# A new order for all engines, planned for eight outstanding loads and stores

## The chip, the core and the metric

The kernel runs on one core of a Trainium2 chip. The core has five engines that each take their instructions strictly in order: TensorE (PE, matmuls, with its weight loads shown as PEld), VectorE (DVE), ScalarE (ACT), GpSimd (POOL) and SyncE (SP, which only issues transfers). Transfers (DMAs) are issued by SP, ACT or POOL and run beside the engines. The metric is the device time of one execution, in microseconds, as the median of several runs; lower is better.

## What is computed

Two operators in a row: causal attention with 16 beacon keys in front, then a feed-forward layer with an ELU.

```python
B, H, S, D, Nb = 8, 8, 576, 64, 16
k_all = concat([beacon_k, k], axis=2); v_all = concat([beacon_v, v], axis=2)
scores = q @ k_all.T / sqrt(D), causal after the beacons
a = exp(scores) / sum(exp(scores))
x = (a @ v_all).transpose(0, 2, 1, 3).reshape(B * S, H * D)      # 4608 x 512
h = x @ w_in                                                       # 512 x 2048
g = where(h > 0, h, exp(h) - 1)
out = g @ w_out                                                    # 2048 x 512
```

Inputs and output are float32; inside, the matmuls take bf16 or fp16.

## The kernel before

The eight batches of attention and the feed-forward layer are interleaved in one program. A batch has four pairs of heads. For a pair (numbers n = 4b + hp) the steps are:

- load k and q (`load_pair`, 288 KB each) or, from batch 3 on, whole rows of tokens (`load_tok`); load the values of the batch (`load_v`) and the beacons (`load_bk`);
- cast them to bf16 (`cast_pair`, on DVE, POOL or ACT) into one of two buffers `sb`;
- bring them into the form that the scores need: PE transposes (`do_T2` for batch 0, `do_T` for batches 1 and 2; tiles `tr2`, `tr`) with copies out on DVE or ACT, or DMA transposes issued by SP (`turn_tok`);
- scores on PE (`do_SC`, tile `sc`, two buffers), exponentials on ACT (`do_exp`, tile `et`), the causal mask on POOL (`do_mask`), value matmuls on PE (`do_AV`, tile `av`), division on DVE (`do_norm`), and the way back into the transposed x by PE (`do_xT`, tile `xt`) or SP (`turn_x`).

The feed-forward layer works through the 4608 tokens in tiles of 128, 128, 256 and then 512. For each tile, sixteen groups of up-projection matmuls (`do_mm1`, tile `hps`; fewer and wider groups cover the small tiles) are followed by the exponential on ACT (`do_e`), a clamp on POOL (`do_clamp`) and the ELU on DVE (`do_join`). The down-projection (`do_plain` for the first 512 tokens, then `do_M` with seven products in place of eight; tile `ops`) is copied out and stored by SP. Both weight matrices come in four pieces of 1 MB each, cast to fp16 by the transfer (`load_w`, issued by POOL, 512 KB as written).

The order of the instructions is not that of the source. Each step is an `Op` with an engine, a due time, a duration and what it needs. The class `Plan` plays through the whole program while it is being built (`Plan.run`), engine by engine in the order of the due times, lets an op wait for what it needs, and then emits the instructions in the order in which they began. Only this order reaches the chip; what waits for what is then held by semaphores. Three tables written out by hand feed it: `KEYS` (the due times), `ENGINES` (one letter for each op that may run on several engines: S, A, P, D for SP, ACT, POOL, DVE) and a few constants. Where PE has nothing to do in the first 30 us of the played time, the planner puts in a filler matmul (`do_fill`, tile `spare`, line L290).

For transfers the planner before knows 16 ring places for each of SP and ACT (`ringSP`, `ringACT`; a large transfer takes four or eight), three queues that share one transfer engine in turn, and a duration and a latency for each kind. The built program has a further rule, in both kernels: the loads and stores issued by SP and ACT take eight completion semaphores (lanes) in turn, in the order in which they are emitted, so the ninth waits at the head of its engine's queue until the first has landed. POOL's loads of the weights have lanes of their own.

Of the kernel before, what the change touches and what calls it, by code (L numbers as in the profile page):

```python
# [22 lines left out]
class Op:  # L23
    def __init__(self, eng, key, dur, fn, deps=(), take=(), give=(), mode=None, lat=0.03, queue=0, parts=1):
        self.eng, self.key, self.dur, self.fn = eng, key, dur, fn
        self.deps, self.take, self.give = [d for d in deps if d is not None], take, give
        self.mode, self.lat, self.queue, self.parts = mode, lat, queue, parts
        self.left, self.after, self.rest = 0, [], parts
        self.lock = fn is not None and (eng, getattr(fn, "func", fn).__name__) in SHARED


class Plan:
    MODE_COST, SLACK = 0.1, 0.1
    ENGS = "PE", "SP", "ACT", "POOL", "DVE"

# [3 lines left out]
    def add(self, *args, **kw):  # L39
        op = Op(*args, **kw)  # L40
        self.ops.append(op)
        return op

    def run(self):
# [15 lines left out]
        free = dict.fromkeys(todo, 0.0)  # L60
        free["DMA"] = 0.0
        mode, lines, turn, port = None, ([], [], []), 0, 0.0
        events, order, now, n_left, tick = [], [], 0.0, len(self.ops), 0
# [12 lines left out]
        while n_left:  # L76
# [11 lines left out]
            for eng, line in todo.items():  # L88
# [3 lines left out]
                if op.left or any(self.slots[t] < op.take.count(t) for t in op.take):  # L92
# [7 lines left out]
                line.pop()  # L100
                for t in op.take:
                    self.slots[t] -= 1
# [19 lines left out]
            while events and events[0][0] <= now + 1e-9:  # L122
# [3 lines left out]
                n_left -= 1  # L126
                for t in op.give:
                    self.slots[t] += 1
# [14 lines left out]
def kernel(  # L143
# [134 lines left out]
    with tc.tile_pool(name="psum", bufs=1, space=bass.MemoryType.PSUM) as psum:  # L278
# [4 lines left out]
            "st": 4, "sb": 2, "ringSP": 16, "ringACT": 16, "vst": 4,  # L283
# [32 lines left out]
        def load(key, dur, fn, deps=(), take=(), issue=0.47, units=1, fixed=True):  # L316
# [4 lines left out]
            ring = ["ring" + on] * units  # L321
            one = add(on, key, issue, fn, deps=deps, take=take + ring)
# [7 lines left out]
            return add("DMA", key, dur, None, deps=[issue], lat=2.1, give=ring, queue=0 if on == "SP" else 2, parts=2 * units)  # L330

        issues = {"SP": [], "ACT": [], "st": [], "vst": []}
        add("SP", -1e6, 0.8, None)
        add("PE", -1e6, 1.3, None, mode=0)

        bks = {}

# [8 lines left out]
        def load_pair(n, is_k, eng):  # L346
# [4 lines left out]
            eng = nc.scalar if n == 0 and not is_k else eng  # L351
# [336 lines left out]
        def do_store(s, m, halves):  # L688
# [12 lines left out]
            "SPSPAPADSPDDDADAADDASPDDDDADAASDDDDDDDDSSDDADDDAAAASPSDSPAPDSAPDDASSPDADSSDDDASSPDADSPSPADAPSPPS"  # L701
            "ADDDSSDDASSPDDSSPDAAAAAAAAPAPSADASPAPSSDSSPAPAPAAAAADAASSPSSPAAAAPAAPADSDAPAAADAASAPSSPAPAADSAPA"
            "DAPADSDSAAAASDSSPAPAAAAAPSPADAASASAAPASPAAPAAAAAASPSDDDAADADDDDDAADDDDADAADDDAAAADDDAAADDDDAADAD"
            "DDAADDDDDADAADDADDDDDDDA"
# [178 lines left out]
        def place(b, a):  # L883
            return 32 * (b - 1) + 8 * a + SHIFT[b]
# [350 lines left out]
```

## Time and profile before

| | |
|---|---|
| median of 3 runs | 351.3 us (350.16 to 351.71) |
| the profiled execution | 351.03 us |
| its span on the core | 349.3 us |
| granted clock of PE over the span | 1.0 |
| HBM read, written | 37.22 MB, 9.44 MB |
| fillers (L290) | 125 |

The profile lists each engine's busy time as a union of its instructions' spans. In rows of groups, the columns are the source line, the engine, the operation, out<-in with shapes, the count, then busy us and mean ns of one, then the idle time of the engine just ahead of them and what ended most of it. Matmuls are pipelined: one takes longer from start to end than the distance to the next, so PE's rate is read from the time that a row of many takes. In a timeline or a list of issues the first column is the start in us, the second the length, and the bracket at the end is the idle time before and what ended it; "SPq" is an instruction that issues a transfer. In the chain of waits each row is a start, a length and what the time was spent on.

### The profile page before, as it was taken

The numbers are of one execution on the slowest core, as the hardware profiler recorded it, in microseconds if no ns is written. First come the engines' busy times: TensorE is split into PE (matmuls) and PEld (weight loads), VectorE is DVE, ScalarE is ACT, GpSimd is POOL, SyncE is SP. The second block draws the span as 40 slices with busy tenths as digits, with TensorE's granted clock in tenths as the row PEclk, the third lists the DMA queues.
The fourth block names the chain that finished last, engine by engine and source line by source line (L and its number), as shares of the span: only waits on it lengthen the run. The fifth ranks groups of instructions, "written<-read, shape, count | busy, mean of one in ns | idle before, by whom it ended". The sixth has DMA issues, their size and how long they took to land.

```text
span 349.3 us, 9404 instructions
## 1 busy us (share of the span) xinstructions
PE 335.4 (96%) x3709; PEld 233.2 (67%) x3709; DVE 240.8 (69%) x468; ACT 216.7 (62%) x331; POOL 206.1 (59%) x372
## 2 busy tenths in 40 slices
PE   7989889999998999999999999999999999999996
PEld 5557787755553685667768887568665667666685
DVE  3456487767677867787777658576667696686872
ACT  2557888757767775866657668676785664352420
POOL 3398799766864886577448575375364574324310
PEclk9999999999999999999999999999999999999999
DMA  7999969999899898999899769947222410310113
GB/s 214 283 256 247 226 145 228 206 189 181 173 183 195 118 214 131 214 193 194 157 176 217 146 142 170 197 101 174 63 54 77 118 33 18 85 63 0 62 62 120
DMA packets 139400, 52.61 MB, mean 151 GB/s; under 512 B 119388, under 2 KB 135772, under 8 KB 139356
## 3 DMA queue, kind: packets, MB, share of 16 engines
q1 hardware_dynamic: 84405, 33.39, 44.1%
q10 hardware_dynamic: 50727, 14.42, 22.2%
q0 software_dynamic: 4224, 4.19, 7.6%
q8 instruction: 29, 0.48, 0.6%
q14 instruction: 15, 0.12, 0.1%
HBM read 37.22 MB, written 9.44 MB: 134 GB/s over the span
## 4 chain that ended last, share of the span: by engine, by line
PE 78%; DMA 8%; DVE 5%; POOL 4%; ACT 1%; issue 1%; SPq 1%; ACTq 0%; POOLq 0%; DVEq 0%
PE hps L581 31%; PE ops L651 26%; PE av L525 8%; PE sc L489 7%; DMA xT<-x 4%; PE ops L659 3%; DMA st<-in_q_dram 2%; DMA st<-in_k_dram 2%; PE spare L290 2%; POOL et L505 2%; PE tr L438 1%; POOL e L592 1%; DVE gt L599 1%; DVE t L617 1%; DVE x L541 1%
## 5 line engine op out<-in xcount | busy, mean ns | idle before, releaser
L592 POOL TENSOR_SCALAR e<-e 128x512 f32<-128x512 f32 x144 | 94.6, 661 | 90.8 <-ACT e L588 89.8
L581 PE MATMUL hps<-xT,w_in 128*128 128x512 f16 (+2 forms) x768 | 141.5, 326 | 0.5 <-DVE xT L304 0.3
L498 ACT ACTIVATE et<-sc 128x736 f16<-128x736 f32 (+4 forms) x128 | 109.6, 889 | 31.3 <-PE sc L489 21.0
L599 DVE SCALAR_TENSOR_TENSOR gt<-e,hps 128x512 f16<-128x512 f32 x144 | 96.4, 681 | 44.8 <-POOL e L592 44.4
L588 ACT ACTIVATE e<-hps 128x512 f32<-128x512 f32 x144 | 85.1, 600 | 64.6 <-PE hps L581 59.0
L581 PEld LDWEIGHTS <-w_in 128*128 128x128 f16 x768 | 66.4, 98 | 45.6 <-issue 4.5
L505 POOL TENSOR_SCALAR_AFFINE_SELECT et<-et 128x256 f16<-128x256 f16 (+4 forms) x160 | 72.5, 472 | 22.9 <-ACT et L498 22.0
L651 PEld LDWEIGHTS <-gt 128*128 128x128 f16 x640 | 61.2, 98 | 13.8 <-issue 1.0
L651 PE MATMUL ops<-w_out,gt 128*128 128x256 f16 x384 | 46.9, 273 | 0.0
L525 PEld LDWEIGHTS <-et 128*128 128x128 f16 (+1 forms) x992 | 36.6, 97 | 7.8 <-issue 2.2
L525 PE MATMUL av<-v,et 128*128 128x65 f16 (+1 forms) x992 | 40.3, 193 | 1.2 <-POOL et L505 0.6
L489 PE MATMUL sc<-qT,kT 64*128 64x80 bf16 (+3 forms) x704 | 36.4, 231 | 2.2 <-ACT et L498 2.1
L489 PEld LDWEIGHTS <-kT 64*128 64x128 bf16 x704 | 21.2, 95 | 19.5 <-issue 16.3
L541 DVE TENSOR_TENSOR x<-av,rl 128x256 f16<-128x256 f32 (+2 forms) x68 | 32.1, 471 | 2.3
L651 PE MATMUL ops<-t,gt 128*128 128x256 f16 x256 | 31.9, 273 | 0.0
L540 DVE RECIPROCAL rl<-av 128x4 f32<-128x4 f32 (+2 forms) x68 | 12.5, 184 | 27.7 <-PE av L525 27.4
L304 POOL CAST st<-st 128x1024 bf16<-128x1024 f32 (+3 forms) x25 | 24.4, 974 | 7.0 <-DMA st<-in_q_dram 5.6
L651 PEld LDWEIGHTS <-s 128*128 128x128 f16 x256 | 24.2, 98 | 4.8 <-DVE s L631 0.2
L684 DVE TENSOR_TENSOR osb<-ops,part 128x512 f32<-128x512 f32 (+1 forms) x27 | 17.0, 630 | 7.4 <-PE ops L651 5.7
L290 PE MATMUL spare<-t 128*128 128x256 f16 x125 | 19.3, 289 | 1.4 <-DVE t L1168 1.3
L651 PE MATMUL ops<-t,s 128*128 128x256 f16 x128 | 16.1, 272 | 0.0
L290 PEld LDWEIGHTS <-t 128*128 128x128 f16 x125 | 12.0, 103 | 6.1 <-issue 1.9
(53 smaller groups left out, 216.9 us busy)
## 6 DMA issues: line engine op xcount, KB each, us to landing
out_dram<-osb SPq DMA_DIRECT2D x32, 256.0 KB, 3.1
vst<-in_v_dram ACTq DMA_DIRECT2D x15, 256.0 KB, 4.6
st<-in_q_dram ACTq DMA_DIRECT2D x14, 256.0 KB, 4.3
st<-in_k_dram SPq DMA_DIRECT2D x10, 288.0 KB, 5.9
st<-in_q_dram SPq DMA_DIRECT2D x9, 288.0 KB, 6.2
st<-in_k_dram SPq DMA_DIRECT2D x10, 256.0 KB, 4.7
w_in<-in_moe_w_in_dram POOLq DMA_DIRECT2D x4, 512.0 KB, 10.3
w_out<-in_moe_w_out_dram POOLq DMA_DIRECT2D x4, 512.0 KB, 8.4
```

The costliest lines, as they stand in the source:

```text
L290: nc.tensor.matmul(out=spare[:, 0:2 * P], lhsT=ones[:, 0:P], rhs=ones, start=True, stop=True)
L304: eng.tensor_copy(out=out, in_=in_)
L489: nc.tensor.matmul(out=sc[:, h, o:o + w], lhsT=kT[D * h:D * h + D, keys_of(n, jc)], rhs=qT[D * h:D * h + D, q0:q0 + w], start=True, stop=T ...
L498: nc.scalar.activation(out=et[:, :, 0:w], in_=scs[n, u][:, :, 0:w], func=AFT.Exp, bias=0.0, scale=float(1.0 / (D ** 0.5)))
L505: nc.gpsimd.affine_select(out=et[:, :, c0:c0 + dw], in_=et[:, :, c0:c0 + dw], compare_op=ALU.is_ge, fill=fill0, base=q0 + NB - keys.start, ...
L525: nc.tensor.matmul(out=av[:, c:c + D + 1], lhsT=ets[n, cut.unit_of[jc, at]][0:m, h, col:col + P], rhs=v16[0:m, jc, 2 * hp + h, 0:D + 1], s ...
L541: nc.vector.tensor_tensor(out=x16s[b % 2][:, blks[0]:blks[0] + nb, P * hp:P * hp + P].rearrange("q i (h d) -> q i h d", d=D), in0=av[:, :, ...
L581: nc.tensor.matmul(out=hps[:, (hi - lo) * j + a - lo:(hi - lo) * j + b - lo], lhsT=w_in16[:, cc, P * fc:P * fc + P], rhs=xT[cc][:, a % RIN ...
L588: nc.scalar.activation(out=e, in_=hpss[tt, i], func=AFT.Exp, bias=0.0, scale=1.0)
L592: nc.gpsimd.tensor_scalar(out=e, in0=e, scalar1=1.0, scalar2=0.0, op0=ALU.min, op1=ALU.max)
L599: nc.vector.scalar_tensor_tensor(out=gt, in0=e, scalar=1.0, in1=h, op0=ALU.subtract, op1=ALU.max)
L651: nc.tensor.matmul(out=bank_of(s, m, slice(half, half + 1))[:, 0], lhsT=a[:, fc, P * half:P * half + P], rhs=B_OF[m][:, fc], start=(first ...
```

## The change

The planner gets the eight lanes, loses the rings, and its tables are written anew. `Plan` has `LANES = 8`; each issue on SP or ACT takes one lane (two where a beacon part is loaded by an instruction of its own) and may begin only when the next lanes in turn are free; the landing gives them back. Start times of the engines come from `BEGIN` in place of two dummy ops. The assumed durations of transfers are raised by some per cent and split finer. All loads of pairs may now go to SP or ACT (`fixed=False`), also those of pair 0, and the rule that loads of one issuing engine keep their order among themselves is dropped (only those that share a set of buffers still do).

```diff
 class Plan:
     MODE_COST, SLACK = 0.1, 0.1
     ENGS = "PE", "SP", "ACT", "POOL", "DVE"
+    BEGIN = {"PE": 1.3, "SP": 0.8, "ACT": 0.8}
+    LANES = 8
...
+    def add_dma(self, issue, lanes, key, dur, **kw):
+        op = self.add("DMA", key, dur, None, deps=[issue], **kw)
+        op.issue, issue.lanes = issue, lanes
         return op
...
-                if op.left or any(self.slots[t] < op.take.count(t) for t in op.take):
+                lanes = [(lane + i) % self.LANES for i in range(op.lanes)]
+                if op.left or any(busy[i] for i in lanes) or any(self.slots[t] < op.take.count(t) for t in op.take):
...
                 line.pop()
+                for i in lanes:
+                    busy[i] = True
+                op.lane, lane = lanes, lane + op.lanes
...
                 n_left -= 1
+                if op.issue is not None:
+                    for i in op.issue.lane:
+                        busy[i] = False
...
-            "st": 4, "sb": 2, "ringSP": 16, "ringACT": 16, "vst": 4,
+            "st": 4, "sb": 2, "vst": 4,
...
+        PAIR, VALS, TOKS, WTS = 0.85, (0.95, 1.4), 1.3, 3.4
...
-            eng = nc.scalar if n == 0 and not is_k else eng
...
         ENGINES = (
-            "SPSPAPADSPDDDADAADDASPDDDDADAASDDDDDDDDSSDDADDDAAAASPSDSPAPDSAPDDASSPDADSSDDDASSPDADSPSPADAPSPPS"
...
+            "ADSDSDSDSDASSDADDAAADAADDDDDDDDSAPADADDADASPDDADDDDSPSDSPSPSADSSDADDSSPDDDSSDADDSSDADASAAPSDSPSA"
...
         KEYS = [
...
-                gots.append(load(key, 0.8, partial(load_pair, n, is_k), deps=() if is_k or n == 0 else "last",
-                                 take=["st"] if is_k else [], issue=0.61, fixed=n == 0))
+                gots.append(load(key, PAIR, partial(load_pair, n, is_k), deps=() if is_k or n == 0 else "last",
+                                 take=["st"] if is_k else [], issue=0.61, fixed=False))
...
-            got = add("DMA", 0, 3.2, None, deps=[got], lat=2.1, queue=1, parts=8)
+            got = add("DMA", 0, WTS, None, deps=[got], lat=2.1, queue=1, parts=12)
...
-        plan.lines = [issues[line] for line in ("SP", "ACT", "st", "vst")]
-        last = add("DMA", 0, 0.7, None)
+        plan.lines = [issues[line] for line in ("st", "vst")]
...
-        last.deps.append(sorted(issues["SP"], key=lambda i: i.key)[2])
```

What this does to the built program, engine by engine:

| | before | after |
|---|---|---|
| fillers on PE | 125 | 106 |
| of these, ahead of the first transposes | 26 | 41 |
| loads issued by ACT | 67 | 25 |
| loads and stores issued by SP | 105 | 147 |
| DMA transposes issued by SP | 80 | 80 |
| pairs of batch 0 loaded ahead of the first values | 2 | 4 |
| POOL: what stands ahead of the first piece of w_in | two pair casts, three value casts, a mask | two pair casts |
| POOL: order of the weight pieces | w_in, w_in, w_out, w_in, w_in, w_out x3 | w_in x4, w_out x4 |
| PE: score pairs, value matmuls and transposes ahead of the first up-projection | those of batch 0 nearly whole and some of batch 1 | a part of those of batch 0 |

The first loads stand so in the new program. SP: beacon k, k of a second pair, beacon k, q and k of the first pair, q of a fourth, values. ACT: k and q of a third pair, q of the second, then a cast of the beacon keys, k of the fourth pair. DVE's first cast is that of the pair whose q and k SP issues fourth and fifth.

More of the change, by code (lines that the diff above doesn't have):

```diff
@@ L59, in run @@
             line.reverse()
-        free = dict.fromkeys(todo, 0.0)
+        free = {e: self.BEGIN.get(e, 0.0) for e in todo}
         free["DMA"] = 0.0
+        busy, lane = [False] * self.LANES, 0
         mode, lines, turn, port = None, ([], [], []), 0, 0.0
-        events, order, now, n_left, tick = [], [], 0.0, len(self.ops), 0
+        events, order, now, n_left, tick = [(t, -1, None) for t in sorted(set(self.BEGIN.values()))], [], 0.0, len(self.ops), 0
         def arrive(o):
@@ L314, in movable, with load @@
             return op
-        def load(key, dur, fn, deps=(), take=(), issue=0.47, units=1, fixed=True):
+        def load(key, dur, fn, deps=(), take=(), issue=0.47, parts=2, lanes=1, fixed=True):
             deps = [issues["new"]] if deps == "last" else deps
@@ L320, in load @@
             fn = partial(fn, eng)
-            ring = ["ring" + on] * units
-            one = add(on, key, issue, fn, deps=deps, take=take + ring)
+            one = add(on, key, issue, fn, deps=deps, take=take)
             if not fixed:
@@ L329, in load @@
             issues["vst" if "vst" in take else "st"].append(issue)
-            return add("DMA", key, dur, None, deps=[issue], lat=2.1, give=ring, queue=0 if on == "SP" else 2, parts=2 * units)
+            return plan.add_dma(issue, lanes, key, dur, lat=2.1, queue=0 if on == "SP" else 2, parts=parts)
         issues = {"SP": [], "ACT": [], "st": [], "vst": []}
-        add("SP", -1e6, 0.8, None)
-        add("PE", -1e6, 1.3, None, mode=0)
         bks = {}
+        PAIR, VALS, TOKS, WTS = 0.85, (0.95, 1.4), 1.3, 3.4
         def load_bk(b, eng):
@@ L925, in plan_v @@
                 key = load_key(f"v{NKC * b + jc}", place(b - 1, 1.8 + 0.4 * jc))
-                got = load(key, 0.85 if b < NV and jc < NKC - 1 else 1.3, partial(load_v, b, jc), take=["vst"], issue=0.95 if jc == 0 or jc == 1 and b < NV else 0.48, units=4 if b < NV and jc < NKC - 1 else 8, fixed=False)
+                got = load(key, VALS[0] if b < NV and jc < NKC - 1 else VALS[1] if jc < NKC - 1 else VALS[1] * 0.65, partial(load_v, b, jc), take=["vst"], issue=0.95 if jc == 0 or jc == 1 and b < NV else 0.48,
+                           lanes=2 if jc == 0 or jc == 1 and b < NV else 1, parts=8 if b < NV and jc < NKC - 1 else 16, fixed=False)
                 v_cast[b, jc] = movable(
@@ L951, in plan_tok @@
                         s = add("SP", (place(b, DMA_AT[1]) + i), 1.25, partial(turn_tok, b, is_k, c + j),
-                                deps=[cast] + last_SC.get(b - 2, []), take=ring4)
-                        turned[b].append(add("DMA", place(b, DMA_AT[1]) + i, 0.6, None, deps=[s], give=ring4, lat=2.1, parts=8))
+                                deps=[cast] + last_SC.get(b - 2, []))
+                        turned[b].append(plan.add_dma(s, 1, place(b, DMA_AT[1]) + i, 0.6, lat=2.1, parts=8))
                     add("NONE", 0, 0.0, None, deps=turned[b][-m:], give=["sb"], lat=0.0)
@@ L1032, in plan_pair @@
                         for blk in blks:
[L1033 removed]
+                            s = add("SP", (at(AT[7])), 1.25, partial(turn_x, b, blk), deps=part.pop(blk))
                             turns.setdefault(b, []).append(s)
[L1035 removed]
+                            done = plan.add_dma(s, 1, at(AT[7]), 0.6, lat=2.1, parts=8)
                             last_X.setdefault(b, []).append(done)
@@ L1158, in plan_super @@
                         freed[mate] = got
-                        st = add("SP", k + 0.1, 0.47, partial(do_store, s, m, halves), deps=[got], take=["ringSP"])
-                        gone.append(add("DMA", k + 0.1, 0.75 if half is None else 0.38, None, deps=[st], give=["ringSP"], lat=2.1 if half is None else 2.0, parts=2))
+                        st = add("SP", k + 0.1, 0.47, partial(do_store, s, m, halves), deps=[got])
+                        gone.append(plan.add_dma(st, 1, k + 0.1, 0.75 if half is None else 0.38, lat=2.1 if half is None else 2.0, parts=2))
                     chain.append(got)
```

18 lines of the change are left out of this document (9 added, 9 removed), and 338 rows, old and new, of the table KEYS.

## The prediction

> **What bounds the kernel now.** I read the busy shares first, then the slices, then TensorE (PE) stage by stage, then the chain of waits of the first stage, then the queues that feed it. From the page:
>
> ```profile
> span 349.3 us, 9404 instructions
> PE 335.4 (96%) x3709; PEld 233.2 (67%) x3709; DVE 240.8 (69%) x468; ACT 216.7 (62%) x331; POOL 206.1 (59%) x372
> ...
> DMA  7999969999899898999899769947222410310113
> ```
>
> PE is busy 96% of the span and no other engine passes 69%. DMA is near full for the first half and idle for the last third. By stages (columns after the stretch: its length, then busy time and count of PE, PEld, DVE, ACT, POOL, then clock, DMA share, GB/s):
>
> ```profile
> 0.00:6.92 6.92, 4.47 (x26) 3.20 (x26) 1.48 (x7) 1.28 (x1) 2.56 (x17) 1.00 0.63 186
> 6.92:36.70 29.78, 26.98 (x367) 19.15 (x368) 17.14 (x45) 17.92 (x25) 20.88 (x31) 1.00 1.12 265
> 36.70:70.00 33.30, 30.25 (x527) 25.70 (x524) 23.62 (x59) 27.09 (x41) 28.19 (x49) 1.00 1.00 199
> 70.00:346.20 276.20, 273.68 (x2797) 185.16 (x2794) 198.55 (x360) 170.18 (x266) 154.42 (x277) 1.00 0.68 132
> ```
>
> From 70 us on PE idles 2.5 of 276 us: there is nothing to win there and, if loads come late, something to lose. Everything open lies before 70 us. The same view for the filler matmuls alone (line L290, which keep PE turning while data is on its way):
>
> ```profile
> 0.00:6.92 6.92, 4.47 (x26) 3.20 (x26) 1.00 0.63 186
> 6.92:36.70 29.78, 14.81 (x99) 8.75 (x99) 1.00 1.12 265
> ```
>
> All of PE's work before 6.92 us is filler, and of the 367 matmuls up to 36.70 us, 99 are. So the start is a wait for data. The chain of waits of this stage (start, length, what):
>
> ```profile
> 0.84 3.33 DMA st<-in_k_dram
> 4.18 8.09 DMA st<-in_q_dram
> 12.35 0.77 DVE st L304
> ...
> 14.86 1.42 PE spare L290 x12
> ...
> 24.45 0.55 PE sc L489 x8
> ...
> 26.88 0.29 PE sc L489 x10
> ...
> 27.38 0.50 PE tr L438 x9
> ```
>
> The first link is a load, the second a load that was issued only when the first had landed (0.84 + 3.33 = 4.17; issue at 4.18). That is the limit the change is about: there are eight completion lanes, and the ninth load or store of SP and ACT waits at the head of its queue until the first is in. The issues show it (start, length of the issue):
>
> ```profile
> 1.25 0.74 SPq L352 DMA_DIRECT2D st<-in_k_dram  x1
> 2.04 0.62 SPq L352 DMA_DIRECT2D st<-in_q_dram  x1
> ...
> 4.18 0.61 SPq L352 DMA_DIRECT2D st<-in_q_dram  x1
> 8.44 0.60 SPq L352 DMA_DIRECT2D st<-in_k_dram  x1
> ```
>
> SP stands from 4.79 to 8.44. The old plan did not know this limit, so its order was made for loads that come earlier than they do.
>
> **The change, part by part.** No operation of the result is added or removed; what changes is every engine's order, the number of fillers (125 to 106), and who issues loads (ACT 67 to 25, SP's loads and stores 105 to 147, SP's transposes 80 in both).
>
> *Where the first up-projection stands.* Before it, the old order has 106 value matmuls (av), 28 more transposes than the new one, and 12 score matmuls of 256 columns, 4 of 240 and 20 of 80 more; the new one has 32 av there. By the chain's rows 28 transposes at 0.50/9 = 0.056 are 1.6 us, 16 wide scores at 0.55/8 = 0.069 are 1.1, 20 narrow ones at 0.29/10 = 0.029 are 0.6; 74 av at the rate of a full group are 2.2:
>
> ```profile
> 291.47 1.46 PE av L525 x48
> ```
>
> ```profile
> 36.71 0.28 PE L581 MATMUL hps<-xT,w_in 128*128 128x128 f16 x2
> 68.54 1.03 PE L581 MATMUL hps<-xT,w_in 128*128 128x256 f16 x8
> ```
>
> The last two rows are the old first and sixteenth group of up-projections. 5.5 us of real work are left for later, so the new kernel breaks even if its first up-projection starts at 36.7 - 5.5 = 31.2 us, as long as the rest runs as closely packed. Now when does it start?
>
> *The first data.* The new order begins with three whole pairs of k and q, spread over both queues; VectorE's first cast wants the pair that SP issues fourth and fifth, 928 KB into SP's queue (32 + 288 + 32 + 288 + 288). What the old trace shows of landings, by the casts that waited for them:
>
> ```profile
> 6.11 0.76 DVE L304 CAST st<-st 128x1152 bf16<-128x1152 f32 x1 [4.51 <-DMA st<-in_q_dram]
> ...
> 6.93 0.68 PE L448 MATMUL tr<-identb,st 128*128 128x128 bf16 x9 [1.20 <-DVE st L304]
> ...
> 8.55 1.14 POOL L304 CAST st<-st 128x1152 bf16<-128x1152 f32 x1 [5.25 <-DMA st<-in_q_dram]
> ...
> 10.24 0.61 POOL L304 CAST v<-vst 128x512 f16<-128x512 f32 x1 [0.54 <-DMA vst<-in_v_dram]
> ...
> 11.51 0.61 POOL L304 CAST v<-vst 128x512 f16<-128x512 f32 x1 [0.66 <-DMA vst<-in_v_dram]
> ```
>
> SP's 608th KB was in at 8.55, its 864th at 11.51, ACT's 832nd at 10.24. The new pair's 928 KB on SP stand beside 864 KB on ACT, so 11.5 is the upper end if the queues share as before and 10.2 the lower; I take 11.0, then 0.76 for the cast: first transposes at about 11.9, against 6.93 now. Fillers cover only part: 26 took 4.47 us (cold), 15 more at 1.42/12 = 0.118 end at 7.5 us, then PE stands for 4.4 us. That loss is wanted: the second, third and fourth pair are then in or nearly in, whereas the old kernel waits for each in turn (8.55 and 12.35 us).
>
> *From the first transposes to the first up-projection.* ACT sets this. In the new order ACT copies, then runs nine exponentials of batch 0 before the score pair whose last part stands just ahead of the up-projection.
>
> ```profile
> 7.70 0.45 ACT L302 ACTIVATE qT<-tr 128x256 bf16<-128x256 bf16 x1 [5.61 <-PE tr L451]
> ...
> 10.90 0.97 ACT L498 ACTIVATE et<-sc 128x960 f16<-128x960 f32 x1 [2.41 <-POOL v L304]
> 12.86 1.94 ACT L498 ACTIVATE et<-sc 128x1024 f16<-128x1024 f32 x2 [0.98 <-PE sc L489]
> ...
> 18.38 1.02 ACT L498 ACTIVATE et<-sc 128x1024 f16<-128x1024 f32 x1 [0.71 <-PE sc L489]
> ```
>
> First exponential 3.2 us after the first transposes (two pairs are cast and transposed by then, and three copies like the first row go ahead on ACT). Then four of 0.97, five of 1.0, two q copies and one xT copy between them (1.3 in all), and 0.8 for a wait where a pair of score tiles needs both buffers. The rows show 0.71 to 0.98 for each such wait; there are three places, and I count one, since in the others ACT still works on the tile before when the first of the pair is written. 3.9 + 5.0 + 1.3 + 0.8 = 11.0; 3.2 before and 0.9 after it for narrow scores and four fillers make 15.1 us from the transposes, near 27.0. I add 1.2 for hand-overs that I did not count, about 0.1 us at each of a dozen steps: 28.2. Bounds: 26.0 (data at 10.2, no slip) and 31 (data at 11.5, slip of 3).
>
> *The weights.* GpSimd issues the first two pieces of w_in after its two casts (1.14 each, from 12.8 on): 15.2 and 16.1 us, now 19.48 and 20.97.
>
> ```profile
> 19.48 0.90 POOL L430 DMA_DIRECT2D w_in<-in_moe_w_in_dram  x1
> ...
> 20.97 0.76 POOL L430 DMA_DIRECT2D w_in<-in_moe_w_in_dram  x1
> ```
>
> ```profile
> w_in<-in_moe_w_in_dram POOLq DMA_DIRECT2D x4, 512.0 KB, 10.3
> ...
> st<-in_q_dram SPq DMA_DIRECT2D x9, 288.0 KB, 6.2
> ```
>
> At 10.3 us to landing, piece one is in at 25.5, before the start at 28.2. A further one follows each 2 to 5 us (512 KB at the 199 to 265 GB/s of the stages, alone or with one other queue), about as each is used. Pieces three and four stand behind masks on GpSimd, hence the slip above; if that cover is gone, every us is paid.
>
> *Up-projections 1 to 16.* The old kernel goes from its first group to its sixteenth in 31.8 us. In the new order PE has 25.5 us of work between first and sixteenth (counted as above, the groups at 0.9 us), ACT 16 exponentials of L588 and 12 of L498.
>
> ```profile
> L498 ACT ACTIVATE et<-sc 128x736 f16<-128x736 f32 (+4 forms) x128 | 109.6, 889 | 31.3 <-PE sc L489 21.0
> L588 ACT ACTIVATE e<-hps 128x512 f32<-128x512 f32 x144 | 85.1, 600 | 64.6 <-PE hps L581 59.0
> ```
>
> 16 x 0.600 + 12 x 0.889 = 20.3, with copies 23. Old PE idle in that stage was 33.30 - 30.25 = 3.1 us; I take the same, so 28.6 us with ACT at 80%, where it now has 27.09 of 33.30 = 81%. Ends: 0 (ACT at 90%) and 6.
>
> *Issues moved from ACT to SP.* 42 x 0.61 = 25.6 us leave ACT's queue over the run, hidden now by ACT's 38% idle time; worth 0, at most 1. On SP a load then stands behind transposes and stores that wait; SP idles most of the run, but what is queued behind a waiting transpose is late by that wait. I take 0 from 70 us on, ends -1 and +3.
>
> **Sum.** 28.2 - 31.2 = -3.0 us; later stages 0; tail of the last supertile the same order of matmuls and stores. The profiled execution took 351.03 us (349.3 of span and 1.7 around it), the runs' median is 351.3: 351.03 - 3.0 = 348.0.
>
> **A rule against it.** The Trainium skill, "SBUF — State Buffer", in its box on VectorE blocking a DMA, says that a load issued from GpSimd is starved while VectorE runs copies in a fast mode. No run here shows that lock by itself, but the 10.3 us to landing for 512 KB of w_in against 6.2 for 288 KB on SP leave room for it; the new order issues w_in amid VectorE's copies too.
>
> **The rivals.**
>
> *A, slower: the start moves as a whole.* SP, VectorE and GpSimd each take things in order. If the pair on SP's queue lands at 13 instead of 11, the cast of a pair that is long in (6.11 in the old trace) waits behind it, the exponentials start 2 us later, GpSimd's casts too, and with them w_in, which stands behind those casts. Priced: start at 31.2 + 2.5 = 33.7, 353.5 us. It decides as soon as the first up-projection starts after 31.2. For it: the first transposes do come 5 us later by my own sum, with the 15.1 us of ACT behind them. Against it: 11.5 is a measured landing for nearly as many bytes. 0.23.
>
> *B, given back on ACT.* PE and ACT have almost equal work in the sixteen groups, so each wait of one is a wait of the other. If ACT gets only 73% full, between the 81% there and the 17.92 of 29.78 = 60% of the stage before, they take 31.5 instead of 28.6 us: 348.0 + 2.9 = 350.9, no change. For it: the new order has no attention of batch 1 to fill in with as early. Against: ACT is freed of load issues. 0.14.
>
> *C, the plan decides little.* If DMA volume alone sets the time up to 70 us, since its share is 1.0 to 1.2 there, both orders end where the bytes do: 351.0. Against: the share was 0.63 in the first 6.92 us, and which bytes come first is what PE waits for. 0.05.
>
> *D, the clock.* The first 26 fillers took 0.17 us each and later ones 0.118, though the clock column says 1.00. If PE's 4.4 us of standing slows it again, the next transposes and scores (some 2 us) take twice as long, half of it on the path: 349.0. 0.05. The Trainium skill, "TensorE: Matmul & The Clock Gate", Part 1, says that about 3.4 us without work halves the clock; by that rule D happens.
>
> **How the numbers follow.** Forecast 0.53 (own range 345 to 349.5), A 0.23, B 0.14, C 0.05, D 0.05. About 0.5%, 1.8 us, is what a measurement tells from no change. Faster: 0.53 and D, 0.58. Same: B and C, with a little of A, 0.21. Slower: the rest of A, 0.21. The range reaches from 344.0 (start at 26, some of the 3.1 us idle saved) to 354.0 (A).
>
> **What would show it.** First transposes near 11.9 and not before 10.9; ACT's first exponential near 15; first up-projection at 28.2, before 31.2; PE idle time from there to the sixteenth group near 3 us; 106 fillers; after 80 us PE never idle for long, and the last stage as long as now. Wrong if PE waits for w_in at the first up-projections, if the first cast ends after 13 us, or if new gaps on PE after 70 us exceed 3 us in all.

## The result, and the profile after

The changed kernel is slower. Its median is 361.1 us (360.33 to 361.64, 4 runs) against 351.3 us for the kernel before (350.16 to 351.71, 3 runs; a fourth took 483.65 us and is left out as slow). The recorded ratio is 1.0301, with a 95% interval from 1.0267 to 1.0335; the two medians alone give 1.028. The profiled execution took 361.64 us, 359.7 of them in the span. The page of the changed kernel, lines as shown of before, with the granted clock and the two hardware queues (q1 is SP's, q10 ACT's):

```profile
span 359.7 us, 9342 instructions
...
PE 337.4 (94%) x3690; PEld 233.3 (65%) x3690; DVE 237.6 (66%) x466; ACT 219.4 (61%) x335; POOL 199.1 (55%) x370
...
PEclk9999999999999989999699999999999999999999
DMA  7899928999799999899989799744403300220213
...
q1 hardware_dynamic: 117973, 42.34, 58.1%
q10 hardware_dynamic: 17159, 5.47, 8.0%
```

Two slices of the clock line are below 9, one from 126 us on and one from 171 us on; in the kernel before none was. The stages of the changed kernel (columns as in the prediction: length, then PE, PEld, DVE, ACT, POOL, clock, DMA share, GB/s), cut at its first transposes and its first up-projection:

```profile
0.00:10.67 10.67, 7.17 (x41) 5.22 (x42) 1.48 (x7) 1.91 (x2) 2.56 (x17) 1.00 0.79 237
10.67:29.39 18.72, 16.64 (x195) 10.96 (x196) 12.11 (x32) 12.07 (x18) 16.08 (x22) 1.00 1.06 203
...
90.00:130.00 40.00, 34.20 (x393) 21.64 (x392) 26.38 (x54) 28.03 (x41) 23.69 (x47) 0.96 1.03 169
130.00:190.00 60.00, 56.88 (x649) 37.42 (x648) 39.52 (x77) 40.03 (x60) 38.27 (x73) 0.94 1.04 170
190.00:359.00 169.00, 163.96 (x1623) 116.87 (x1620) 115.36 (x206) 91.78 (x146) 79.47 (x147) 1.00 0.45 99
```

PE alone, in the kernel before, over nearly the same stretches:

```profile
90.00:130.00 40.00, 38.48 (x439) 1.00 0.96 173
130.00:190.00 60.00, 59.54 (x656) 1.00 1.02 183
```

The start came out near the forecast, the stretch from 90 to 190 us did not: PE stands for 8.9 us there (40.00 - 34.20 + 60.00 - 56.88), where it stood for 2.0, and its clock falls.

PE's order can be followed as work done: count its matmuls in order, without fillers, at their undisturbed rate, and read when each kernel has done so many us of them. The table is worked out from the two traces in this way.

| PE's work done, us | before, at us | after, at us | after is ahead by |
|---|---|---|---|
| 40 | 64.8 | 61.5 | 3.3 |
| 70 | 94.8 | 91.2 | 3.6 |
| 90 | 116.4 | 114.2 | 2.2 |
| 100 | 126.1 | 128.0 | -1.9 |
| 140 | 165.5 | 166.6 | -1.1 |
| 150 | 174.9 | 183.6 | -8.7 |
| 310 | 331.8 | 341.1 | -9.3 |

The change wins 3.6 us at the start and loses 12.9 behind it, 4.1 at one place and 7.6 at another. These are the two places in the timeline (start, length, instruction, and the idle time before it with what ended it):

```profile
121.50 1.04 PE L664 MATMUL ops<-t,gt 128*128 128x256 f16 x8
124.75 2.46 PE L594 MATMUL hps<-xT,w_in 128*128 128x512 f16 x8 [2.21 <-DVE gt L612]
...
171.04 0.52 PE L502 MATMUL sc<-qT,kT 64*128 64x256 bf16 x14
174.29 1.09 PE L538 MATMUL av<-v,et 128*128 128x65 f16 x12 [2.73 <-DVE gt L612]
...
123.38 0.72 DVE L320 CAST st<-st 128x1024 bf16<-128x1024 f32 x1 [5.26 <-DMA kT<-st]
124.02 1.87 DVE L612 SCALAR_TENSOR_TENSOR gt<-e,hps 128x512 f16<-128x512 f32 x3
...
172.32 0.61 POOL L320 CAST st<-st 80x512 bf16<-80x512 f32 x1 [3.18 <-DMA kT<-st]
172.90 1.19 POOL L605 TENSOR_SCALAR e<-e 128x512 f32<-128x512 f32 x2
...
173.54 1.29 DVE L612 SCALAR_TENSOR_TENSOR gt<-e,hps 128x512 f16<-128x512 f32 x2 [5.26 <-POOL e L605]
```

Read from the bottom of each: PE waits for a join (`gt`) on DVE. At 124 us three joins stand behind a cast of tokens; at 173 us the join waits for a clamp on POOL that stands behind such a cast. The cast waits for a DMA transpose to land, which gives back one of the two `sb` buffers. Behind each wait PE has work again but at a lower clock:

```profile
118.00:122.00 4.00, 3.64 (x31) 1.00 1.28 173
122.00:126.00 4.00, 1.79 (x11) 0.99 0.95 192
126.00:130.00 4.00, 4.00 (x18) 0.58 0.75 154
...
172.00:176.00 4.00, 1.49 (x15) 0.71 0.85 170
176.00:180.00 4.00, 4.00 (x29) 0.50 1.04 209
180.00:184.00 4.00, 4.00 (x68) 0.93 0.77 174
```

PE's busy time in these six rows by what the clock lacks of 1.00 comes to 4.4 us, most of it 4.00 x 0.42 and 4.00 x 0.50. So the wait of 2.21 us was followed by 1.7 us lost to the clock, the one of 2.73 us by 2.7 us.

### The profile page after: what moved, and what is told of

It reads as the page before. It is cut to its first block, busy times and chain, and to the rows that moved or that the text cites. A ratio compares the mean times of both kernels' runs of the same rounds, so it can differ in the third digit from the quotient of the medians.

```text
span 359.7 us, 9342 instructions
## 1 busy us (share of the span) xinstructions
PE 337.4 (94%) x3690; PEld 233.3 (65%) x3690; DVE 237.6 (66%) x466; ACT 219.4 (61%) x335; POOL 199.1 (55%) x370
## 4 chain that ended last, share of the span: by engine, by line
PE 65%; DMA 17%; DVE 5%; SPq 3%; POOL 2%; issue 2%; ACT 1%; ACTq 0%; POOLq 0%; DVEq 0%
PE hps L594 27%; PE ops L664 21%; DMA kT<-st 6%; PE av L538 6%; PE sc L502 5%; PE ops L672 4%; DMA st<-in_q_dram 4%; DMA vst<-in_v_dram 3%; DMA xT<-x 2%; DVE gt L612 2%; SPq L400 2%; DMA out_dram<-osb 1%; DMA st<-in_k_dram 1%; POOL et L518 1%; PE tr L451 1%
## 5 line engine op out<-in xcount | busy, mean ns | idle before, releaser
L605 POOL TENSOR_SCALAR e<-e 128x512 f32<-128x512 f32 x144 | 92.8, 649 | 87.1 <-ACT e L601 85.8
L511 ACT ACTIVATE et<-sc 128x1024 f16<-128x1024 f32 (+4 forms) x128 | 109.4, 889 | 38.2 <-PE sc L502 28.9
L601 ACT ACTIVATE e<-hps 128x512 f32<-128x512 f32 x144 | 83.9, 600 | 60.5 <-PE hps L594 55.2
L518 POOL TENSOR_SCALAR_AFFINE_SELECT et<-et 128x256 f16<-128x256 f16 (+4 forms) x160 | 70.5, 460 | 33.3 <-ACT et L511 31.6
L664 PEld LDWEIGHTS <-gt 128*128 128x128 f16 x640 | 62.1, 99 | 13.3 <-issue 1.5
L538 PEld LDWEIGHTS <-et 128*128 128x128 f16 (+1 forms) x992 | 36.8, 98 | 10.3 <-issue 5.2
L664 PE MATMUL ops<-t,gt 128*128 128x256 f16 x256 | 32.7, 282 | 0.1
L320 POOL CAST st<-st 128x1024 bf16<-128x1024 f32 (+3 forms) x21 | 19.4, 924 | 21.9 <-PE tr L464 8.1
L306 PE MATMUL spare<-t 128*128 128x256 f16 x106 | 17.6, 306 | 3.3 <-DVE t L1182 1.3
L320 DVE CAST st<-st 128x1152 bf16<-128x1152 f32 (+3 forms) x12 | 8.6, 726 | 14.1 <-DMA st<-in_k_dram 8.3
## 6 DMA issues: line engine op xcount, KB each, us to landing
w_out<-in_moe_w_out_dram POOLq DMA_DIRECT2D x4, 512.0 KB, 12.9
```

The source lines that it names most:

```text
L306: nc.tensor.matmul(out=spare[:, 0:2 * P], lhsT=ones[:, 0:P], rhs=ones, start=True, stop=True)
L320: eng.tensor_copy(out=out, in_=in_)
L511: nc.scalar.activation(out=et[:, :, 0:w], in_=scs[n, u][:, :, 0:w], func=AFT.Exp, bias=0.0, scale=float(1.0 / (D ** 0.5)))
L518: nc.gpsimd.affine_select(out=et[:, :, c0:c0 + dw], in_=et[:, :, c0:c0 + dw], compare_op=ALU.is_ge, fill=fill0, base=q0 + NB - keys.start, ...
L538: nc.tensor.matmul(out=av[:, c:c + D + 1], lhsT=ets[n, cut.unit_of[jc, at]][0:m, h, col:col + P], rhs=v16[0:m, jc, 2 * hp + h, 0:D + 1], s ...
L601: nc.scalar.activation(out=e, in_=hpss[tt, i], func=AFT.Exp, bias=0.0, scale=1.0)
```

## The experiments

Four theories were told apart: **S**, SP's queue is too full, since 42 loads moved to it; **C**, casts that wait hold up joins and clamps in order; **D**, the 16 DMA engines are full from 60 us on and the new order has left them work undone; **B**, two buffers are too few. These letters are not those of the prediction's rivals. All ratios are against the kernel before, run on the same chip; the changed kernel itself stands at 1.030.

### Loads moved back from SP to ACT, and the reverse

The order on every engine and the plan stay; only the issuing engine of 39 loads is another (names: q, k or v, batch, block).

```diff
+        MOVED = "q34 k31 k32 k34 q40 q41 q42 q43 k44 q51 q53 q54 k51 k54 q60 ... v70 v71 v74".split()
...
-            fn = partial(fn, eng)
+            fn = partial(fn, nc.scalar if name_of(fn) in MOVED else eng)
```

> The changed kernel, its plan and the order on every engine kept, but the 39 loads of batches 3 to 7 that the change moved from ACT's queue to SP's are issued on ACT again. Theory S (a filled SP queue makes the DMA transposes, then the casts that wait for a buffer, then the joins late): SP's issue time from 118 to 163 us falls from 20 to about 15 of every 20 us, the gaps of PE at 122 and 171 us (2.5 and 2.9 us) are gone and the clock stays at 1.00 behind them: 349 to 353 us, since the start's lead of 3.5 us is kept. Rival T (the casts that the change put on DVE in batch 4, or the eight-lane bound, are the cause): the gaps stay, 359 to 362 us. Rival A (ACT is now the engine that is short): new gaps of PE that end on exp or e of ACT, 355 us or more.

357.8 us, ratio 1.0208 (1.0154 to 1.0262): three of the ten us come back, less than S said. The wait at 171 us is gone; at 121 us PE still stands, for another reason:

```profile
118.30 0.84 ACT L520 ACTIVATE et<-sc 128x800 f16<-128x800 f32 x1
122.22 0.39 ACTq L397 DMA_DIRECT2D st<-in_q_dram  x1
122.66 1.08 ACT L610 ACTIVATE e<-hps 128x512 f32<-128x512 f32 x2 [3.52 <-DMA out_dram<-osb]
```

A load at the head of ACT's queue waits until a store has landed; that the two share a lane is read from the eight-lane rule. The exponential behind the load, which is in no need of that, waits 3.5 us too. So a load is not free on ACT either.

> As the run before it, but only the 15 of those loads that are planned from 113 to 162 us go back to ACT. Theory S: nearly the same time, 349 to 354 us, as the stalls come from SP's queue in that stretch. If the queue before 113 us also counts (SP has 17 of 20 us there), the gap at 109 us and some of the one at 122 us stay, 354 to 358 us. Rival T: 359 to 362 us.

With 15 loads: 357.3 us, 1.0217 (1.0166 to 1.0269), the same. Here again the first wait stays and the second goes.

> As the run with 39 loads back on ACT, but the load of q's block 1 of batch 4 stays on SP: on ACT it waited 3.5 us for its DMA lane, and ACT's exp and e behind it, which made a gap of 3.3 us at 121 us. If that one load was what kept the run from 349 to 353 us, this one gets there: the gap at 121 us falls below 1 us, the clock stays at 1.00, 351 to 354 us. Rival (SP's transposes are late here whichever engine issues the loads): a gap over 2 us stays there, ended by a cast or a transpose, 356 to 359 us.

356.9 us, 1.0198 (1.0160 to 1.0236). In the profiled execution (353.9 us) the wait at 121 us is down to 0.8 us and the clock stays at 1.00 there, but the single load was not what kept the time up: ACT loses 3.0 us at 135 us to another load of q that waits for a transpose.

The reverse edit in the kernel before:

```diff
-            fn = partial(fn, eng)
+            fn = partial(fn, nc.sync if name_of(fn) in MOVED else eng)
```

> The kernel before, its plan and order kept, with the same 39 loads issued on SP instead of ACT, so 39 x 0.57 = 22 us more in SP's queue from 60 to 240 us. Theory S: late transposes and gaps of PE appear in a kernel that has no other part of the change, with a lower clock behind them: 355 to 362 us. Rival T: 351 us, within 1 us.

351.6 us, 1.0031 (1.0002 to 1.0060). By its trace SP issues for 17.8 of the 20 us from 100 to 120 and 18.5 from 140 to 160, nearly as full as in the changed kernel (18.8 and 18.7), and it costs 1 us. A full queue alone is not the cause; S falls as a theory of the whole.

### Casts and buffers

```diff
+        LATER = {(4, True, 2): 119.61, (5, True, 4): 161.06}
+        for op in plan.ops:
+            if getattr(op.fn, "func", None) is cast_tok:
+                op.key = LATER.get(op.fn.args[:3], op.key)
```

> The changed kernel with two instructions moved and nothing else: the cast of k's blocks 2 and 3 of batch 4 stands four joins later on DVE, the cast of k's block 4 of batch 5 stands behind three more clamps on POOL. These are the two casts that the joins behind the gaps of PE at 122 and 171 us waited for. Theory C (a cast that waits for its buffer holds up, in order, the joins and clamps behind it; that is what turns SP's lateness into time of PE): the two gaps shrink below 1 us and the clock stays at 1.00 behind them; 2.5 + 1.7 us and 2.9 + 3.2 us come back, less what the transposes, now a little later, cost: 352 to 356 us. Rival (PE would have stood anyway, as scores wait for the late transposes): the gaps move to a wait for kT or qT, 358 to 362 us.

364.1 us, 1.0393 (1.0364 to 1.0423): slower still, though both waits went and the clock stayed at 1.00 from 90 to 260 us. What PE waits for from 100 to 195 us (total, times, longest), changed kernel first, then this one:

```profile
PE av L538 <- DVE gt L612: 2.7, 1, 2.7
PE hps L594 <- DVE gt L612: 2.2, 1, 2.2
PE sc L502 <- DMA kT<-st: 1.0, 1, 1.0
```

```profile
PE hps L594 <- DVE x L554: 2.8, 2, 1.4
PE hps L594 <- DMA xT<-x: 1.8, 1, 1.8
PE ops L664 <- DVE osb L320: 1.7, 1, 1.7
PE av L538 <- POOL et L518: 1.5, 1, 1.5
PE sc L502 <- DMA qT<-st: 1.2, 2, 0.9
```

Two waits have become many, some directly for transposes. The cast is the place where lateness shows, not where it comes from: C falls. Over 100 to 195 us PE does 999 matmuls in each of the two kernels, changed kernel first:

```profile
100.00:195.00 95.00, 86.98 (x999) 0.95 1.06 173
```

```profile
100.00:195.00 95.00, 83.24 (x999) 1.00 0.97 170
```

The changed kernel lets PE stand for 8.0 us and loses some 4.4 to the clock (86.98 x 0.05); with the casts moved PE stands for 11.8 us at a whole clock. Keeping the clock up won nothing, so what it takes in the changed kernel can't simply be added to the other costs.

Both edits together:

> Both edits: 38 loads back on ACT and the two casts later. Theories S and C together: no gap of PE over 1.5 us behind 30 us, clock 1.00, the lead of the start kept: 348 to 352 us. If small gaps from the denser plan of batch 4 remain (1 to 4 us in all behind 90 us): 352 to 355 us.

360.1 us, 1.0279 (1.0242 to 1.0317). Slower than the loads alone.

```diff
-            o = b16s[...] = stage.tile([P, G, 2, D], BF16, tag="sb", name="st16", bufs=2)
+            o = b16s[...] = stage.tile([P, G, 2, D], BF16, tag="sb", name="st16", bufs=3)
...
-            e = es[tt, i] = melt.tile([P, TTS], FP32, tag="e", name="e", bufs=NE)
+            e = es[tt, i] = melt.tile([P, TTS], FP32, tag="e", name="e", bufs=3)
```

> The changed kernel with three buffers instead of two for the cast tokens (sb), and three instead of four for e, to make room; orders and issues are kept. The casts behind the stalls at 122 and 171 us waited for such a buffer. Theory B (the two buffers are the link: a cast can't start before the transposes two before it have landed): both stalls shrink below 1 us, 350 to 354 us. Theories S and D (transposes leave and land late in any case): the casts start sooner, but their transposes are still behind SP's queue: 356 to 361 us, the wait moves on to the transposes.

359.3 us, 1.0258 (1.0204 to 1.0312): 1.5 us, so the buffers are a small part, and B falls as a theory of the whole. The edit also takes away one of the four e buffers; what that costs was not told apart.

What one wait costs by itself, in the kernel before:

```diff
-            copy_on(eng, ...)
+            for _ in range(9 if (b, is_k, c) == (5, False, 0) else 1):
+                copy_on(eng, ...)
```

> The price of one hold by itself: the kernel before, in which one cast on DVE (q's blocks 0 and 1 of batch 5, 0.7 us, at 148.5 us) is done nine times over, so DVE is held for 5.8 us more. If a late join costs only its own gap: 351 + 2 to 4 us, clock 1.00 behind it. If the clock falls behind the gap, as it did at 122 and 171 us in the changed kernel: a gap of 2.5 to 4 us, a granted clock of 0.6 to 0.85 over the 10 us behind it, and 351 + 4 to 7 us.

357.6 us, 1.0204 (1.0174 to 1.0234), 6.9 us more. The timeline, then the windows of PE:

```profile
155.97 2.29 PE L582 MATMUL hps<-xT,w_in 128*128 128x512 f16 x5 [5.62 <-DVE gt L600]
...
146.54 8.19 DVE L304 CAST st<-st 128x1024 bf16<-128x1024 f32 x9
```

```profile
150.00:156.00 6.00, 0.38 (x3) 0.78 0.32 76
156.00:160.00 4.00, 4.00 (x12) 0.50 0.80 162
```

DVE is held for 8.2 us and PE stands for 5.6, then runs 4 us at half its clock, 2 us more. The order of before makes up less than 1 us of the 7.6 in the 190 us that follow.

### Fewer packets, the same bytes

What the DMA engines had moved, first in the kernel before, then in the changed one. The first row of each is up to the moment when PE has done 40 us of work (64.8 and 61.5 us), the second from 50 to 60 us, the third from 60 to 170 us:

```profile
DMA packets 18931, 14.85 MB, mean 229 GB/s; under 512 B 8170, under 2 KB 15850, under 8 KB 18922
...
DMA packets 2786, 2.27 MB, mean 227 GB/s; under 512 B 1159, under 2 KB 2327, under 8 KB 2785
...
DMA packets 69298, 19.74 MB, mean 179 GB/s; under 512 B 66867, under 2 KB 68771, under 8 KB 69283
```

```profile
DMA packets 13254, 12.29 MB, mean 200 GB/s; under 512 B 3174, under 2 KB 10854, under 8 KB 13246
...
DMA packets 1029, 1.31 MB, mean 131 GB/s; under 512 B 70, under 2 KB 582, under 8 KB 1028
...
DMA packets 69510, 20.92 MB, mean 190 GB/s; under 512 B 66615, under 2 KB 68151, under 8 KB 69497
```

From 60 to 170 us both kernels move the same number: 69,298 and 69,510 packets in 110 us, 630 and 632 per us, nearly all under 512 bytes. What is not moved by 60 us is still missing at 170 (3,048 packets, then 2,836). In bytes the changed kernel makes up 1.2 of 1.9 MB in that time, so the ledger is one of packets. At equal work the changed kernel is 5,677 packets behind, 9.0 us at 630 per us, an estimate; PE, which is 3.3 us ahead, would run into it. If that is the cause, larger packets must give the time back. The edit fetches whole rows of 512 neighbouring floats, so the bytes, issues and orders stay; q, k and v then hold other rows of the input.

```diff
+            if b >= 3:
+                eng.dma_start(out=vst[r0:r0 + n].rearrange("p h d -> p (h d)"),
+                              in_=v[b].rearrange("h s d -> (h s d)").rearrange("(s f) -> s f", f=DM)[lo:lo + n])
+                return
             eng.dma_start(out=vst[r0:r0 + n], in_=v[b, :, lo:lo + n, :].rearrange("h s d -> s h d"))
```

> The changed kernel, all orders, issues and bytes kept, but the loads of v of batches 3 to 7 fetch whole rows of 2 KB (512 neighbouring floats of the input for each partition) instead of 8 pieces of 256 bytes: the values are those of other rows, and some 20,000 of the 139,400 packets are gone. Theory D (the 16 DMA engines, at 620 to 700 packets per us from 60 us on, are the limit behind the start; the change leaves them idle from 50 to 60 us and is 5,700 packets behind at equal work of PE, which it has to make up at 90 to 200 us): with spare DMA time the deficit is made up at no cost, transposes land sooner, the stalls at 122 and 171 us shrink below 1 us each: 346 to 352 us. Theory S (SP's time to issue, which this leaves as it is): the stalls stay, 358 to 362 us.

355.9 us, 1.0165 (1.0106 to 1.0225): 5 us come back, half of the loss. The wait at 171 us is gone; one of 2.71 us is left that ends at 118.91, with a DMA transpose of x, and the clock is at 0.50 over the next 4 us.

> The same edit in the kernel before. Theory D: its transfers are just in time already, PE has gaps of only 0.7 to 2 us, so little comes of it: 349 to 351 us. If DMA also bounds the kernel before, 345 to 348 us.

351.1 us, 1.0018 (0.9986 to 1.0049): nothing, as D says.

> The same edit in the changed kernel with 38 loads back on ACT, which took 356.9 us. Theory D: 345 to 350 us, and near the run without the loads moved. If SP's issue and the DMA engines each take a part, this one is faster than the run without the loads moved by 2 us or more.

355.2 us, 1.0129 (1.0049 to 1.0209): the loads on ACT add 0.7 us to the gain of the rows, within the scatter. The same with q and k too (`load_tok` edited in the same way):

> As the run with v in whole rows, and q and k of batches 3 to 7 in whole rows too, so that q, k and v hold other rows of the input: some 60,000 of the 139,400 packets are gone, with every order, issue and byte kept. v alone took the time from 361 to 355.9 us. Theory D: with this much free time of the DMA engines transposes and loads land soon after they are issued; both stalls go, 347 to 351 us. Theory S (SP's issue time, 95 to 165 us): what is left of the loss stays, 354 to 358 us, with the stall at 116 to 124 us still there.

352.3 us, 1.0060 (1.0025 to 1.0094): 8 to 9 of the ten us are back. SP still issues for 18.8 and 18.7 of the 20 us from 120 and from 140 us on, the stretch where S put the cause. PE in this run:

```profile
90.00:130.00 40.00, 38.33 (x471) 1.00 0.84 180
130.00:190.00 60.00, 56.11 (x648) 1.00 0.91 193
```

The control:

> The control: the kernel before with the same 60,000 packets fewer. Theory D as told here (the kernel before has its transfers just in time, so the gain in the changed kernel is what the change had lost): 349 to 351.5 us. If freeing the DMA engines makes any order faster by itself: 343 to 347 us, and the 9 us that the changed kernel gained prove little.

350.1 us, 0.9991 (0.9960 to 1.0023). Fewer packets are worth nothing to the order of before; what they give to the new order is what the new order had lost.

> q, k and v of batches 3 to 7 in whole rows (60,000 packets fewer) in the changed kernel with 38 loads back on ACT. The rows alone took 352.3 us, the loads on ACT alone 356.9 us. If DMA time and SP's issue time are the two causes and nothing else: no gap over 1.5 us, 347 to 349.5 us, under the kernel before by the lead of the start. If the loads on ACT cost ACT what they save SP: 351 to 354 us.

352.5 us, 1.0073 (1.0034 to 1.0111). With DMA time to spare, SP relieved of 38 loads gives nothing more. So a full SP queue hurt here only while transfers were late already, and the gains of D and S do not add up; that both bring the same transposes sooner is argued, not shown.

The Trainium skill, "DMA: Bandwidth & Descriptors", section "Why small descriptors are slow (HBM only)", puts a fixed cost of some three cycles on every packet, 27% at 256 bytes. The direction agrees: from 60 to 170 us the two hardware queues took 94.8 + 11.5 = 106% of the 16 engines' time with 69,510 packets and 79.9 + 7.1 = 87% with 34,173, for about the same 21 MB.

### The hole at 50 to 60 us, and a try at a faster order

```diff
+        for op in plan.ops:
+            if getattr(op.fn, "func", None) is load_v and op.fn.args[:2] == (1, 1):
+                op.key = 52.99
```

> The changed kernel with one load moved: on SP's queue the load of v's block 1 of batch 1, which stands there from 45 to 54 us until its buffer is free, goes behind the five loads of q and k that wait behind it although their buffers are free, so some 1.4 MB go out 9 us sooner and the DMA engines do not idle from 50 to 60 us (131 GB/s there). Theory D, and the deficit comes from that hole: the packets at equal work of PE rise at 60 us, the stalls behind it shrink, 353 to 358 us. If the deficit comes from the order as a whole, since the loads of batches 3 and 4 still wait for the buffers that casts give back: 359 to 362 us. If the moved traffic makes that block of v late in its turn, it costs 1 to 2 us: 361 to 363 us.

360.7 us, 1.0294 (1.0245 to 1.0343): no change. The five loads do go out sooner (13,802 packets by 60 us, 12,865 without the edit), but by 90 us the counts are equal again, 30,728 and 30,749. So that hole alone is not where the deficit comes from. That the next loads wait for the buffers which later casts give back, and that the deficit belongs to the order of loads and casts as a whole, is argued, not shown.

The last run takes the order of before in the new planner, with due times and queues of loads, casts, transposes and stores shifted so that the plan still holds when transfers take 10 to 20% longer than assumed:

> A try at a faster kernel: the order of before, with keys of loads, casts, transposes and stores shifted by some us and some loads given to the other queue, so that the plan still holds with DMA transfers 10 to 20 per cent longer and issues on SP 0.15 us longer than planned. If slack against late transfers is worth anything to the kernel before: 346 to 349 us. If that kernel has slack enough: 350 to 352 us.

355.0 us, 1.0118 (1.0072 to 1.0165). It is slower than the kernel before. No run beat both kernels; the one that the findings point to, larger packets for the same data, needs another layout of q, k and v, and wasn't tried.

## Why the prediction was wrong, step by step

*The start* came out as forecast in its sum, in part by luck. Forecast: first transposes near 11.9 and not before 10.9, ACT's first exponential near 15, first up-projection at 28.2, 28.6 us from there to the sixteenth. Measured: 10.67, 13.93, 29.39, and 56.41 - 29.39 = 27.0 us with 27.02 - 24.97 = 2.1 us of idle PE (3.1 was taken). The rows:

```profile
9.85 1.43 DVE L320 CAST st<-st 128x1152 bf16<-128x1152 f32 x2 [8.26 <-DMA st<-in_k_dram]
...
10.67 0.68 PE L461 MATMUL tr<-identb,st 128*128 128x128 bf16 x9 [2.24 <-DVE st L320]
...
13.93 0.95 ACT L511 ACTIVATE et<-sc 128x960 f16<-128x960 f32 x1
...
29.39 1.06 PE L594 MATMUL hps<-xT,w_in 128*128 128x128 f16 x16
```

The first cast had its data at 9.85, 0.35 us below the lower bound, so the transposes came 1.2 us early; the 15.1 + 1.2 us from there to the up-projection were 18.7, 2.4 more, so the up-projection came 1.2 us late. By the prediction's own sum that leaves 29.4 - 31.2 = -1.8 in place of -3.0. The sixteen groups gave 1.6 us back (27.0 for 28.6), which the sum had not counted on, and the lead of 3.3 us at 40 us of work, 3.6 at 70, agrees with -3.0 because these errors cancel. The upper bound of 31 adds up to 30.4 only (11.5 + 0.76 + 15.1 + 3). The weights did not hold PE up: w_in took 8.8 us to land (10.3 before), and PE has no idle time just before 29.39.

*The step that failed* is "I take 0 from 70 us on, ends -1 and +3" in the part on issues moved from ACT to SP, which the sum carries on as "later stages 0". Measured: +12.9 us, from 3.6 us ahead at 70 us of work to 9.3 behind at 310. The moved issues themselves were not far off that end of +3: 39 loads back on ACT brought 3 us. Its premise that SP idles most of the run does not hold where it mattered: from 80 to 180 us SP issues for 71.5 of 100 us in the kernel before and for 85.3 in the changed one. What was put at nothing without a reason is the time of the transfers that the new order puts off; with larger packets 8 to 9 of the ten us came back, and the kernel before gained nothing from the same edit.

The prediction read that DMA is near full in the first half and that its share is 1.0 to 1.2 up to 70 us, and drew no price from it for the time behind. It also said that from 70 us on there was "if loads come late, something to lose", and stopped at +3, a number without a row. When both kernels had run 61.5 us, the changed one had moved 13,254 packets and the one before 16,224; the difference at 630 per us is 4.7 us. That is an estimate, and the prediction could have bounded it from the order of the loads, since the kernel before had no slack (PE idle 2.5 us in 276) to take it.

The price of a wait was missing too. The prediction knew the drop of the clock as its rival D, for the start only, at 0.05. It came at 124 and 174 us instead and took 4.4 us. In the kernel before one wait of 5.6 us cost 6.9 us with its clock; in the changed kernel, as the run with the later casts shows, nothing was won by keeping the clock up. How much of the loss is the clock's is therefore not shown.

*The rivals of the prediction.* A (the start moves as a whole) fell at 29.39, below its 31.2. B fell: the sixteen groups took less than forecast, not more. C, that DMA volume sets the time, had the right resource and the wrong place: not up to 70 us, but behind it. D did not happen at the start of the changed kernel: PE stood for 2.24 us in place of 4.4, and the clock stayed at 1.00 over the next 4 us. That was close: in nine of the runs with its order a pause of 2.41 to 3.26 us at the same place was followed by a clock of 0.60 to 0.74. The prediction's sign of being wrong, new gaps of PE after 70 us above 3 us in all, is what happened: 289.00 - 275.03 = 14.0 us against 2.5.

```profile
70.00:359.00 289.00, 275.03 (x2858) 0.98 0.70 132
```

*What stays open.* With 60,000 packets fewer the new order takes 352.3 us and the old one 350.1, though by the same count of PE's work the new one is 1 to 3 us ahead up to 115 us. So some 3 to 5 us of its loss, an estimate, are neither DMA time nor SP's loads. The 2.2 us between the two also hold some 1.6 us lost to the clock at the start of that run, ahead of this: after a pause of 2.75 us it is 0.66 over 4 us and 0.91 over the next 4. Its four runs with a mean clock of 0.998 and more took 349.4 to 351.9 us, the six others 351.7 to 353.9. PE's other waits there are for x from DVE and for its transposes; their cause was not settled. Nor was it tried which part of the order of loads makes the deficit.

## What to carry to other kernels

When a resource is full for a long stretch, compare two orders by how much of its work each has done when the stretch begins, at equal work of the engine that sets the end; here a lead of 3.6 us, won with transfers put off that were worth an estimated 9.0 us, was more than paid back. Follow a wait back to what is late, and test by making that thing faster in both kernels: moving the instruction at which the wait showed only moved the wait. Count the clock behind a wait as well: standing for 5.6 us was followed by 2 us lost to the clock in the kernel before.

## Not expected of the hardware

- The clock of PE falls after short pauses. Over all profiled runs, with the idle time before a matmul as the profile gives it (ends of matmuls are modelled): of 10 pauses of 1.65 to 1.85 us none was followed by a clock below 1.00 over the next 4 us; of 14 pauses of 2.07 to 2.48 us 8 were followed by 0.57 to 0.74 and 6 by 1.00; all 12 of 2.71 us and more were followed by 0.50 to 0.77. The Trainium skill, "TensorE: Matmul & The Clock Gate", Part 1, speaks of an idle window of about 3.4 us that runs freely; the halving agrees, the length does not, the measurement decides, and here pauses from 2.07 us on were at risk.
- From 95 to 125 us the DMA engines passed 612 to 680 packets per us in five kernels, whichever queue they came from: 98% of the engines' time in SP's queue and 12% in ACT's in the changed kernel, 58% and 43% in the kernel before.
- Issuing a DMA transpose takes SP 1.2 us as a rule, twice as long as a load, and at times much longer: in the changed kernel two took 3.38 us together at 120.71, the first of them 2.07. Whether the queue then waits for the engines or for a lane was not told apart.

```profile
118.95 0.58 SPq L387 DMA_DIRECT2D st<-in_beacon_k_dram  x1
...
120.71 3.38 SPq L400 DMA_TRANSPOSE qT<-st  x2
```
